# Splitting the weight conversion into parts that are queued behind subtractions and masks, deferring the split of group 2's x, and sharing the decays of k between two engines

## The chip, the core and the metric

The kernel runs on one core of one Trainium2 chip. The metric is the device time of one execution in microseconds. TensorE (PE) multiplies matrices, VectorE (DVE) and ScalarE (ACT) do elementwise work, GpSimd (POOL) does little here, and nearly all transfers are issued from SyncE's queue (SP). Each engine takes its instructions in order.

## The reference

Two stages follow each other. The first is a retention layer: per batch and head a 64 x 64 state decays by gamma in every step, takes in an outer product of k and v, and is read by q. The second is a feed-forward block with Silu on the 3072 tokens that come out.

```python
batch, n_heads, seq, head_dim = (4, 8, 768, 64)
gamma = 1.0 - 2.0 ** (-5.0 - np.arange(H))
for t in range(S):
    state = gamma * state + einsum('bhd,bhde', k[:, :, t], v[:, :, t])
    y[:, :, t] = scale * einsum('bhd,bhde->bhe', q[:, :, t], state)
h = x @ w_in                 # 3072 x 512 by 512 x 2048
out = (h * sigmoid(h)) @ w_out
```

The listing is shortened; q, k and v are float32 and the two weights are float64.

## The kernel before

**Units and visits.** The sequence is cut into 6 chunks of 128 tokens. A unit n is a pair of chunk c and batch b, n = 4c + b, and there are 24. `visit(m)` does three steps of a pipeline: it transposes k and q of unit m (`stage_t`, with copies out of PSUM on ScalarE at L338), computes scores and state products of unit m-1 (`stage_s`, `stage_a`, `finish_a`, `scale_q`), and the output y of unit m-2 (`stage_y`, `finish_y`). In `finish_a` VectorE multiplies the scores by a mask of decays (am, L370), and forms mid and the new state (L378, L382). `scale_q` multiplies the transposed q by its decays gq (L327). When a chunk begins, `next_chunk` multiplies gq by a step on GpSimd (L276). `scale_k` multiplies k by its decays: for units below 12 as eight pieces of 64 columns on ScalarE (L316), from 12 on as one instruction on VectorE (L320).

**Splits.** A float32 operand is multiplied as three parts (high, scaled low, and a mixed one), so each product of x and w is three matmuls per 128 rows. The four units of a chunk make one group c of x, 512 tokens. `finish_y` copies y out of PSUM (ys, L429, on ScalarE, for groups 0 to 2), and `split_x` makes the three parts: one on ScalarE (L440), two on VectorE (L443, L444). Group 2's ys are also written to memory (yd, L431), because its x is built a second time later.

**Weights.** w_in comes in 16 slices w_0 to w_15 (128 columns each), w_out in 16 more. A slice is loaded as 64-bit words (`load_w`, two slices ahead, in two buffers), and `convert_w` turns it into float32: ScalarE takes an absolute value (ca, L192), VectorE does six steps (L194, L196, L199, L201, L203, L206; here cs, ca, cs, cp, cp and the last add). `split_w` then makes three parts: wi on ScalarE (L116), wil on VectorE (L118), wi on ScalarE (L120), wi on VectorE (L121). `take_w` runs both for the next slice.

**Products.** `product_in(c, f)` multiplies group c with slice f: eight matmuls into bank ha and four into hb. ScalarE copies ha (L512), VectorE subtracts hb (L513), ScalarE applies Silu (L517), and `put_g` writes g to memory one product later. The g tiles and the ys tiles share three buffers (tag hs). The PSUM banks for ha, hb and for the transposed k come from a ring of three (`turn`), so a new transpose of k waits until the L513 that read the bank three turns earlier is done.

**Order.** Visits 0 to 9 come first, with slice 0 taken after visit 3 and slice 1 after visit 7. Then come the products (0,f) and (1,f) for f = 0 to 3; slice f+2 is taken at each (0,f), and visit 10+f follows (1,f). This makes four "periods" of two products and one visit. After them come (0,f), (1,f), (2,f-4) in turn, then the rest. TensorE's order is written out by hand as in the program; on the other engines a recording layer orders what is recorded, and `tc.issue_after` keeps instructions behind a named one. `held`, `evac`, `copied` and `taken_out` hold the last x rounding, transposed copy, ha copy and subtraction, to be named there.

**Output stage.** From about 375 us on, g is read back, split, and multiplied with w_out: for each of the six groups, 16 slices f by four batches b, three matmuls each, gm to ob, gh and glo to oa. A group ends with L648 (ScalarE copies ob) and L653 (VectorE scales oa and subtracts the copy), and a store. All eight banks are used by one group, so the next group's first matmuls wait for these.

Of the kernel before, what the change touches and what calls it, by code (L numbers as in the profile page):

```python
# [12 lines left out]
FP32 = mybir.dt.float32  # L13
# [18 lines left out]
def kernel(  # L32
# [77 lines left out]

    def split_w(f, w32, name, factor):

        w = w_slot(f, name)
        lo = conv.tile([128, 512], FP32, tag="wl", name=f"{name}l_{f}")
        with tc.issue_after(held[0] if f >= NF - 4 else evac[0]):
            nc.scalar.activation(out=w[:, 0, :], in_=w32, func=AF.Copy, scale=HALF * factor)  # L116
        high = w[:, 0, :].bitcast(FP32)
        nc.vector.scalar_tensor_tensor(out=lo, in0=w32, scalar=factor, in1=high,  # L118
                                       op0=ALU.mult, op1=ALU.subtract)
        nc.scalar.activation(out=w[:, 1, :], in_=lo, func=AF.Copy, scale=1.0 / EPS)  # L120
        nc.vector.scalar_tensor_tensor(out=w[:, 2, :], in0=high, scalar=EPS, in1=lo,  # L121
                                       op0=ALU.mult, op1=ALU.subtract)
        return w

# [46 lines left out]
    def convert_w(i):  # L171
# [12 lines left out]
        if not wide:  # L184
            return t
        words = t.rearrange("p (c w) -> p c w", w=2)
# [4 lines left out]
        with tc.issue_after(evac[0]) if evac else ExitStack():  # L191
# [12 lines left out]
                                       in1=p.bitcast(FP32), op0=ALU.mult, op1=ALU.mult)  # L204
        w = s.bitcast(FP32) if i < NF else conv.tile([128, DM], FP32, tag="wl", name=f"cw_{i}")
        nc.vector.tensor_tensor(out=w, in0=s.bitcast(FP32), in1=p.bitcast(FP32), op=ALU.add)  # L206
        return w

    evac, held, w_sb = [], [], {}
    taken = [0]  # L210

    def take_w(after=None):
        i = taken[0]
        taken[0] += 1
        if i >= 2 * NF:
            return
        with tc.issue_after(after) if after else ExitStack():
            w32 = convert_w(i)
        if i < NF:
            w_sb[i] = split_w(i, w32, "wi", scale)  # L220
        else:
            nc.sync.dma_start(out=wo_dram[i - NF], in_=w32)

# [51 lines left out]
    def next_chunk():  # L275
        nc.gpsimd.tensor_tensor(out=gq, in0=gq,  # L276
                                in1=step[:, :HP].unsqueeze(2).to_broadcast([128, HP, C]),
                                op=ALU.mult)


    xt, kt, qt, am = {}, {}, {}, {}
    behind_next = []
    taken_out, copied = [], []
    state, steps_of = {}, {}
# [23 lines left out]
    def scale_k(n):  # L308
        if 0 <= n < len(units):
            t = kqv["k"][n]  # L310
            if units[n][0] == NC - 1:
                t = t[:D]
            if n < 3 * B:

                for h in range(H):
                    nc.scalar.activation(out=t[:, h, :], in_=t[:, h, :], func=AF.Copy,  # L316
                                         scale=gk[:, units[n][0], h : h + 1])
                return
            g = gk[: t.shape[0], units[n][0], :].unsqueeze(2).to_broadcast([t.shape[0], H, D])
            nc.vector.tensor_tensor(out=t, in0=t, in1=g, op=ALU.mult)  # L320

    def scale_q(n):
        c, b = units[n]
        if c > 0 and b == 0:
            next_chunk()
        t, g = (x if c > 0 else x[:, :, D:] for x in (qt[n], gq))
        nc.vector.tensor_tensor(out=t, in0=t, in1=g, op=ALU.mult)  # L327
# [38 lines left out]
    def finish_a(n, sc, sums):  # L366

        c, b = units[n]
        am[n] = one.tile([128, 2, HP, D], FP32, tag="am", name=f"am_{n}")
        mask = nc.vector.tensor_tensor(out=am[n], in0=sc, in1=decay, op=ALU.mult).ins  # L370
        mid = one.tile([128, HP, D], FP32, tag="mid", name=f"mid_{n}", bufs=2)
        steps_of[n] = state.get(b), mid

        with tc.issue_after(mask):
            if c == 0:
                nc.scalar.copy(out=mid, in_=sums[:, 0])
            else:
                nc.vector.tensor_tensor(out=mid, in0=state[b], in1=sums[:, 0], op=ALU.add)  # L378
            if c < NC - 1:
                state[b] = one.tile([128, HP, D], FP32, tag="state", name=f"state_{n}",  # L380
                                    bufs=B + 2)
                nc.vector.tensor_tensor(out=state[b], in0=mid, in1=sums[:, 1], op=ALU.add)  # L382
# [51 lines left out]
    def split_x(c, b, y, raw):  # L434
        x = [xt[c][:, i, :, ts(b, C)] for i in range(3)]
        if raw is None:
            xh, xl = (t.rearrange("p a (o t) -> p o a t", o=2) for t in x[:2])
        else:
            (xh, xl), y = x[:2], raw
        held[:] = [nc.scalar.activation(out=xh, in_=y, func=AF.Copy, scale=HALF).ins]  # L440

        def rest():
            nc.vector.tensor_tensor(out=xl, in0=y, in1=xh.bitcast(FP32), op=ALU.subtract)  # L443
            nc.vector.scalar_tensor_tensor(out=x[2], in0=x[1].bitcast(FP32),  # L444
# [3 lines left out]

        if c > LATE:
            behind_next.append(rest)  # L450
        else:
            rest()
# [18 lines left out]
    def visit(m):  # L471

        first, mid, last = (0 <= m - i < len(units) for i in range(3))
        if first:
            stage_t(m)
# [8 lines left out]
        if mid:  # L484
            stage_a(m - 1, sc)
            with tc.issue_after(taken_out[0]) if taken_out else ExitStack():
                finish_a(m - 1, sc, sums)
            scale_q(m - 1)
        if m == 0:
# [14 lines left out]
    def product_in(c, f):  # L504
# [9 lines left out]
        with tc.issue_after(taken_out[0]):  # L514
            while behind_next:
                behind_next.pop()()
        nc.scalar.activation(out=hs, in_=hs, func=AF.Silu)  # L517
# [27 lines left out]
    def w_out(f):  # L545
        wo[f] = split_w(f, w_got.pop(f), "wo", 1.0)
        get_w(f + 2)
# [25 lines left out]
    for m in range(EARLY + 2):  # L573
        visit(m)
        if m in (3, 7):
            take_w()

# [24 lines left out]
    for n, (c, f) in enumerate(steps):  # L602
        product_in(c, f)
        if (c, f) in takes:
            take_w(taken_out[0] if n >= len(pairs + three) else None)
        put_g(1)
# [15 lines left out]
    for c in range(NC):  # L622
# [8 lines left out]
        for f in range(NF):  # L631
# [6 lines left out]
            for b in range(B):  # L638
                gh, glo, gm = (t[:, i, ts(b, C)] for i in range(3))
                oa, ob = acc[b]  # L640
                nc.tensor.matmul(ob, lhsT=gm, rhs=wo[f][:, 2, :], start=first_, stop=last)  # L641
                nc.tensor.matmul(oa, lhsT=gh, rhs=wo[f][:, 0, :], start=first_, stop=False)  # L642
                nc.tensor.matmul(oa, lhsT=glo, rhs=wo[f][:, 1, :], start=False, stop=last)  # L643
        for b in range(B):
            oa, ob = acc[b]
            o = one.tile([128, DM], FP32, tag=("kt", "qt")[b % 2], name=f"o_{c}_{b}",
                         bufs=(2, 3)[b % 2])
            nc.scalar.copy(out=o, in_=ob)  # L648

            n = 2 if (c, b) == (NC - 1, B - 1) else 1  # L650
            for i in range(n):
# [3 lines left out]
                                               op1=ALU.subtract)  # L655
                queue = nc.sync if c == NC - 1 else nc.scalar
                queue.dma_start(out=out[ds(b * S + c * C, C), cols], in_=o[:, cols])

# [29 lines left out]
```

## Time and profile before

The kernel took 645.5 us (median of 8 runs, 644.44 to 648.83). The profiled execution took 645.66 us; its span, first to last instruction, is 642.9 us, and the mean granted TensorE clock 0.991.

| | busy us | share of the span |
|---|---|---|
| PE | 614.1 | 96% |
| weight loads (PEld) | 507.6 | 79% |
| DVE | 420.2 | 65% |
| ACT | 308.9 | 48% |
| POOL | 11.8 | 2% |

The page's second part cuts the span into 40 slices of 16.1 us, where a digit is a share in tenths. A window view gives, for a stretch of time, each engine's busy time and the granted clock (1.00 is full speed). A timeline row reads: start, length, engine, line, operation, output <- input, and in brackets how long the engine sat idle before it and what released it. A row's length includes the time until its result is written, so two rows in succession overlap a little; what an engine can do per microsecond is read from the distance between starts. Idle time of an engine that does not set the end costs nothing.

| where | us |
|---|---|
| TensorE waits for the q of unit 8 until | 43.24 |
| product (0,0) starts | 54.91 |
| product (0,1) | 64.63 |
| product (0,2) | 73.25 |
| product (0,3) | 83.76 |
| product (0,4) | 97.53 |
| last matmul of the program starts | 637.97 |

### The profile page before, as it was taken

The numbers are of one execution on the slowest core, as the hardware profiler recorded it, in microseconds if no ns is written. First come the engines' busy times: TensorE is split into PE (matmuls) and PEld (weight loads), VectorE is DVE, ScalarE is ACT, GpSimd is POOL, SyncE is SP. The second block draws the span as 40 slices with busy tenths as digits, with TensorE's granted clock in tenths as the row PEclk, the third lists the DMA queues.
The fourth block names the chain that finished last, engine by engine and source line by source line (L and its number), as shares of the span: only waits on it lengthen the run. The fifth ranks groups of instructions, "written<-read, shape, count | busy, mean of one in ns | idle before, by whom it ended". The sixth has DMA issues, their size and how long they took to land.

```text
span 642.9 us, 13556 instructions
## 1 busy us (share of the span) xinstructions
PE 614.1 (96%) x5440; PEld 507.6 (79%) x5440; DVE 420.2 (65%) x725; ACT 308.9 (48%) x618; POOL 11.8 (2%) x70
## 2 busy tenths in 40 slices
PE   5787979999999999999999999999999999999997
PEld 3676767888888888888877888888788888888885
DVE  1788799769987766666789787364554635464631
ACT  7987766656755455444465884231312221322311
POOL 2100000000000000000000000000000000000000
PEclk9998989999999999999999999999999999999999
DMA  9986878536586756665468674243342524332301
GB/s 200 195 184 163 233 185 239 164 125 192 169 257 163 217 161 199 187 196 180 164 227 269 209 229 133 97 157 105 120 142 66 186 77 132 131 117 81 131 0 66
DMA packets 123215, 103.65 MB, mean 161 GB/s; under 512 B 80016, under 2 KB 88464, under 8 KB 123152
## 3 DMA queue, kind: packets, MB, share of 16 engines
q1 hardware_dynamic: 120272, 97.54, 52.2%
q10 hardware_dynamic: 2880, 5.24, 2.2%
q8 instruction: 42, 0.69, 0.5%
q14 instruction: 21, 0.17, 0.1%
HBM read 66.06 MB, written 36.70 MB: 160 GB/s over the span
## 4 chain that ended last, share of the span: by engine, by line
PE 80%; DVE 6%; ACT 5%; SPq 4%; DMA 2%; issue 2%; ACTq 0%; DVEq 0%; POOLq 0%
PE ha L508 25%; PE hb L508 12%; PE oa L642 6%; PE o L642 6%; PE o L643 6%; PE o L641 6%; PE oa L643 6%; PE ob L641 6%; SPq L144 3%; PE y L394 2%; DVE o L653 2%; PE sc L362 1%; ACT o L648 1%; PE sc L352 1%; ACT kf L316 1%
## 5 line engine op out<-in xcount | busy, mean ns | idle before, releaser
L508 PE MATMUL ha<-xt,wi 128*128 128x512 f32 x768 | 192.3, 392 | 0.7 <-DVE g L513 0.7
L508 PEld LDWEIGHTS ha<-xt,wi 128*128 128x128 f32 x768 | 142.6, 188 | 31.8 <-DVE g L513 1.5
L562 DVE TENSOR_TENSOR gs<-gr,gs 128x512 fp32r<-128x512 f32 x96 | 62.2, 685 | 87.4 <-ACT gs L560 87.4
L560 ACT ACTIVATE gs<-gr 128x512 fp32r<-128x512 f32 x96 | 53.6, 621 | 130.7 <-issue 130.0
L508 PE MATMUL hb<-xt,wi 128*128 128x512 f32 x384 | 103.1, 390 | 0.8 <-ACT g L512 0.8
L513 DVE TENSOR_TENSOR g<-g,hb 128x512 f32<-128x512 f32 x96 | 65.6, 684 | 43.4 <-ACT g L512 31.5
L517 ACT ACTIVATE g<-g 128x512 f32<-128x512 f32 x96 | 60.7, 633 | 64.9 <-DVE g L513 64.8
L508 PEld LDWEIGHTS hb<-xt,wi 128*128 128x128 f32 x384 | 71.6, 188 | 16.9 <-ACT g L512 1.8
L642 PE MATMUL oa<-wo,gs 128*128 128x512 f32 x192 | 75.4, 393 | 0.6 <-DVE o L653 0.2
L642 PE MATMUL o<-wo,gs 128*128 128x512 f32 x192 | 74.8, 389 | 0.0
L643 PE MATMUL oa<-wo,gs 128*128 128x512 f32 x192 | 74.7, 389 | 0.0
L641 PE MATMUL o<-wo,gs 128*128 128x512 f32 x192 | 74.7, 389 | 0.0
L643 PE MATMUL o<-wo,gs 128*128 128x512 f32 x192 | 74.7, 389 | 0.0
L641 PE MATMUL ob<-wo,gs 128*128 128x512 f32 x192 | 74.7, 389 | 0.0
L512 ACT ACTIVATE g<-ha 128x512 f32<-128x512 f32 x96 | 56.8, 592 | 31.3 <-PE ha L508 25.2
L563 DVE SCALAR_TENSOR_TENSOR gs<-gs 128x512 fp32r<-128x512 f32 x96 | 62.1, 683 | 0.0
L642 PEld LDWEIGHTS oa<-wo,gs 128*128 128x128 f32 x192 | 36.0, 188 | 10.1 <-DVE o L653 2.6
L641 PEld LDWEIGHTS ob<-wo,gs 128*128 128x128 f32 x192 | 36.0, 188 | 7.7
L641 PEld LDWEIGHTS o<-wo,gs 128*128 128x128 f32 x192 | 36.0, 188 | 7.6
L643 PEld LDWEIGHTS o<-wo,gs 128*128 128x128 f32 x192 | 36.0, 188 | 7.6
L642 PEld LDWEIGHTS o<-wo,gs 128*128 128x128 f32 x192 | 36.0, 188 | 7.5
L643 PEld LDWEIGHTS oa<-wo,gs 128*128 128x128 f32 x192 | 36.0, 188 | 7.3
(81 smaller groups left out, 665.8 us busy)
## 6 DMA issues: line engine op xcount, KB each, us to landing
gd<-g SPq DMA_DIRECT2D x96, 256.0 KB, 2.9
gr<-gd SPq DMA_DIRECT2D x96, 256.0 KB, 2.7
wf<-in_moe_w_out_dram SPq DMA_DIRECT2D x16, 512.0 KB, 3.9
out_dram<-o ACTq DMA_DIRECT2D x20, 256.0 KB, 2.1
wf<-in_moe_w_in_dram SPq DMA_DIRECT2D x16, 256.0 KB, 3.6
wf<-in_moe_w_in_dram SPq DMA_DIRECT2D x32, 128.0 KB, 3.9
kf<-in_k_dram SPq DMA_DIRECT2D x16, 256.0 KB, 5.4
qf<-in_q_dram SPq DMA_DIRECT2D x16, 256.0 KB, 4.6
```

The lines of the kernel that those rows point to most:

```text
L144: nc.sync.dma_start(out=t, in_=src[b, :, ds(c * C, C)].rearrange("h t d -> t h d"))
L394: i = nc.tensor.matmul(yp[ts(e, D), o, a, :], lhsT=lhsT, rhs=rhs, start=(e, o) not in started, stop=True, skip_group_check=True).ins
L508: nc.tensor.matmul(hb if i == 2 else ha, lhsT=w_sb[f][:, i, ts(kk, 128)], rhs=xt[c][:, i, kk, :], start=kk == 0 and i != 1, stop=kk == KIN ...
L512: copied[:] = [nc.scalar.activation(out=hs, in_=ha, func=AF.Copy, scale=ONE_E).ins]
L513: taken_out[:] = [nc.vector.tensor_tensor(out=hs, in0=hs, in1=hb, op=ALU.subtract).ins]
L517: nc.scalar.activation(out=hs, in_=hs, func=AF.Silu)
L560: nc.scalar.activation(out=t[:, 0, :], in_=g, func=AF.Copy, scale=HALF)
L562: nc.vector.tensor_tensor(out=t[:, 1, :], in0=g, in1=high, op=ALU.subtract)
L563: nc.vector.scalar_tensor_tensor(out=t[:, 2, :], in0=t[:, 1, :].bitcast(FP32), scalar=-1.0 / EPS, in1=high, op0=ALU.mult, op1=ALU.add)
L641: nc.tensor.matmul(ob, lhsT=gm, rhs=wo[f][:, 2, :], start=first_, stop=last)
L642: nc.tensor.matmul(oa, lhsT=gh, rhs=wo[f][:, 0, :], start=first_, stop=False)
L643: nc.tensor.matmul(oa, lhsT=glo, rhs=wo[f][:, 1, :], start=False, stop=last)
```

## The change

It has six parts.

1. `split_w` becomes a generator that pauses before its first VectorE step, and the last add of `convert_w` becomes a function of its own. `take_w` has a new argument: with parts = 2 (the periods) the last add and the first rounding are put in a list that runs behind the next subtraction, and the rest behind the next mask; with parts = 1 (the following products up to (2,3)) add and split run behind the next subtraction; with 0 all runs at once as before.
2. Slice 1 is taken after visit 8 instead of 7, behind the mask of that visit.
3. The two VectorE parts of group 2's x are also put behind the next subtraction.
4. The k of units 0, 2, 4 and 6 is scaled on VectorE, that of 12 and 13 on ScalarE; n = 1, 3, 5, 7 and 8 to 11 stay on ScalarE.
5. `next_chunk` runs on ScalarE, in four pieces of 128 columns, at the start of the visit.
6. In the output stage, for all groups but the last, the three matmuls come in the order oa, oa, ob; ScalarE copies and scales oa, and VectorE subtracts ob.

```diff
-    def split_w(f, w32, name, factor):
+    def split_w(f, w32, name, factor, to):
-        w = w_slot(f, name)
+        to[f] = w = w_slot(f, name)
...
         high = w[:, 0, :].bitcast(FP32)
+        yield
         nc.vector.scalar_tensor_tensor(out=lo, in0=w32, scalar=factor, in1=high,
...
-        return w
...
+        def rounded():
+            w = (s.bitcast(FP32) if i < NF else
+                 conv.tile([128, DM], FP32, tag="wl", name=f"cw_{i}"))
+            nc.vector.tensor_tensor(out=w, in0=s.bitcast(FP32), in1=p.bitcast(FP32), op=ALU.add)
+            return w
+
+        return rounded
...
-    def take_w(after=None):
+    def take_w(after=None, parts=0):
...
         with tc.issue_after(after) if after else ExitStack():
-            w32 = convert_w(i)
-        if i < NF:
-            w_sb[i] = split_w(i, w32, "wi", scale)
+            rounded = convert_w(i)
+
+        def finish():
+            w32 = rounded()
+            if i < NF:
+                split = split_w(i, w32, "wi", scale, w_sb)
+                if parts == 2:
+                    next(split)
+                    behind_mask.append(split)
+                else:
+                    list(split)
+            else:
+                nc.sync.dma_start(out=wo_dram[i - NF], in_=w32)
+
+        if parts:
+            behind_next.append(finish)
         else:
-            nc.sync.dma_start(out=wo_dram[i - NF], in_=w32)
+            with tc.issue_after(after) if after else ExitStack():
+                finish()
...
     def next_chunk():
-        nc.gpsimd.tensor_tensor(out=gq, in0=gq,
-                                in1=step[:, :HP].unsqueeze(2).to_broadcast([128, HP, C]),
-                                op=ALU.mult)
+        for a in range(HP):
+            nc.scalar.activation(out=gq[:, a, :], in_=gq[:, a, :], func=AF.Copy,
+                                 scale=step[:, a : a + 1])
...
-            if n < 3 * B:
+            if n in (1, 3, 5, 7) or 2 * B <= n < 3 * B + 2:
...
         mask = nc.vector.tensor_tensor(out=am[n], in0=sc, in1=decay, op=ALU.mult).ins
+        masked[:] = [mask]
...
-        if c > LATE:
+        if c > LATE or c == LATE and y is not None:
             behind_next.append(rest)
...
+        if mid and m > 1 and units[m - 1][1] == 0:
+            next_chunk()
...
+            with tc.issue_after(masked[0]):
+                while behind_mask:
+                    list(behind_mask.pop(0))
             scale_q(m - 1)
...
-                behind_next.pop()()
+                behind_next.pop(0)()
...
-        if m in (3, 7):
-            take_w()
+        if m in (3, EARLY):
+            take_w(masked[0] if m == EARLY else None)
...
-            take_w(taken_out[0] if n >= len(pairs + three) else None)
+            take_w(taken_out[0], 2 if n < len(pairs) else int(n < len(pairs + three)))
...
+                todo = [(oa, gh, 0), (oa, glo, 1), (ob, gm, 2)]
+                for o, g, i in todo if c < NC - 1 else todo[2:] + todo[:2]:
+                    nc.tensor.matmul(o, lhsT=g, rhs=wo[f][:, i, :], start=first_ and i != 1,
+                                     stop=last and i != 0)
...
+            if c < NC - 1:
+                nc.scalar.activation(out=o, in_=oa, func=AF.Copy, scale=ONE_E)
+                nc.vector.tensor_tensor(out=o, in0=o, in1=ob, op=ALU.subtract)
+                nc.scalar.dma_start(out=out[rows, :], in_=o)
+                continue
```

## The prediction

> **What bounds it now.** First the 40 slices of 16.1 us on the page:
>
> ```profile
> PE   5787979999999999999999999999999999999997
> DVE  1788799769987766666789787364554635464631
> PEclk9998989999999999999999999999999999999999
> ```
>
> TensorE is at nine tenths or more from slice 7 on, so time can be won almost only before about 108 us. Next, who TensorE waits for before 130 us:
>
> ```profile
> PE kp L336 <- DMA kqv<-in_k_dram: 5.1, 3, 2.2
> ...
> PE kp L336 <- DVE g L513: 3.7, 2, 3.1
> PE y L394 <- ACT ys L429: 3.3, 2, 2.5
> ...
> PE hb L508 <- ACT g L512: 0.8, 1, 0.8
> ```
>
> (us in all, times, longest.) DMA waits belong to the opening, where loads arrive one after another; the others are queueing in VectorE and ScalarE. Third, the stretches between the first and the fifth product of group 0 (start:end, length, then busy us of PE, PEld, DVE, ACT, POOL; granted clock, DMA share, GB/s):
>
> ```profile
> 48.00:54.90 6.90, 3.93 (x132) 3.45 (x130) 5.81 (x11) 5.69 (x15) 1.13 (x2) 0.75 0.86 195
> 54.90:64.60 9.70, 8.83 (x168) 7.35 (x160) 8.66 (x17) 6.99 (x12) 0.09 (x1) 1.00 0.56 142
> 64.60:73.25 8.65, 8.65 (x167) 7.38 (x160) 6.82 (x13) 6.09 (x18) 0.09 (x1) 1.00 0.78 219
> 73.25:83.76 10.51, 9.14 (x167) 7.23 (x161) 9.19 (x18) 7.87 (x19) 0.09 (x1) 1.00 0.72 198
> 83.76:97.53 13.77, 10.55 (x166) 8.69 (x160) 12.67 (x23) 7.88 (x15) 1.13 (x2) 0.88 0.82 209
> ```
>
> A period is two products (4 x 1.36 us each, that is 5.44) and a visit (3.05 from the undisturbed one, 70.20 to 73.25): 8.5 us. The second period achieves that, the fourth takes 13.8, because VectorE is late there. Fourth, the timelines of VectorE and of TensorE at that stall (start, length, then the wait in brackets):
>
> ```profile
> 89.34 1.42 DVE L443 TENSOR_TENSOR xt<-ys,xt 128x512 fp32r<-128x512 f32 x1
> 90.68 0.68 DVE L203 SCALAR_TENSOR_TENSOR cp<-wf,cp 128x512 f32<-128x512 uint32 x1
> 91.28 0.68 DVE L444 SCALAR_TENSOR_TENSOR xt<-xt 128x512 fp32r<-128x512 f32 x1
> 91.89 0.67 DVE L513 TENSOR_TENSOR g<-g,hb 128x512 f32<-128x512 f32 x1
> ```
> ```profile
> 92.61 1.12 PE L336 MATMUL kp<-ident,kf 128*128 128x128 f32 x4 [3.11 <-DVE g L513]
> ```
>
> The L513 subtraction of (0,3) had its matmuls by 86.8 but stood behind mask, state, decays, a split and a conversion step. It frees the PSUM bank of the next transposes, so TensorE sat 3.11 us. A shorter such case: at 50.90 the y products waited 2.49 us for an L429 copy queued on ScalarE behind w_1's two roundings (L116, L120), which waited for VectorE.
>
> **What is there to win.** The five waits after 47 us are 2.49, 0.48 (L352 for L382), 0.79, 0.58 and 3.11: 7.45 us. Then the clock. The Trainium skill (TensorE: Matmul & The Clock Gate, What's actually happening) ties the half clock to about 3.4 us of idleness; by that alone these gaps cost nothing more. The trace differs: after the 2.49 and 3.11 us gaps the granted clock was 0.57 in 50.90 to 54.91 and 0.55 in 92.61 to 96.00. The visit at 92.61 took 4.92 instead of 3.05 us (1.87 lost), the one at 50.90 took 4.01 from its y products on where 71.17 to 73.25 took 2.08 (1.93, of it 0.48 counted). So 3.3 more by the row, 10.8 together; I take the row.
>
> **Part by part.**
> *Anchor.* The first 35 issues on the SP queue keep their order. At 43.24 TensorE waits for the q of unit 8 by DMA (0.60), so nothing before 43.24 can come earlier; I keep the visit there, with its 1.14 us of issue, to 47.31. Four k scalings moved to VectorE here (n = 0, 2, 4, 6) save ScalarE 8 steps, 1.9 us, and cost VectorE 0.60 each: both before the anchor or beside loads, worth 0; without that cover at most 0.60 each.
>
> *w_1 taken one visit later, behind the mask.* Its conversion leaves the visits of 42 to 50 us: the ys copy then follows the y products at once and the mask of unit 7 comes at 47.1 instead of 49.62. Gone: 2.49 and most of 0.48 and of 1.93. The visit takes 3.05 and some slack: (0,0) starts at 51.3 instead of 54.91, 3.6 won. Given back: between the state of unit 7 (ends near 49.0) and the last split of unit 7's x, VectorE now has 16 instructions. By the distance of their starts in its timeline (91.28 to 91.89 for one) they are eleven of 0.60, two of 0.33, cs 0.34, ca 0.42 and cp 0.43: 8.45, and 8.7 with some 0.1 between dependent neighbours (80.51 to 81.23). They end at 57.7; product (1,0) wants that third part at 51.3 + 2.72 + 1.81 = 55.8. So TensorE ends (1,0) at 57.7 + 0.91 = 58.6 instead of 60.54: 1.9 left. The w_3 load on SP also no longer stands 4.9 us (for L203 at 47.66) ahead of k, q of unit 10 and v of 9; these come 6 us earlier, which is slack.
>
> *Slices in parts, halves of group 2's x.* No operation and no semaphore is added, only order: what waits behind the mask is wil, and behind the next subtraction the splits of x, needed a period or more later ((2,0) is the first reader of x of group 2). The ys tile is held some 3 us longer, and is wanted again only by the next visit's ys. In the built order VectorE goes mask, mid, wil, state, wi, q decay, subtraction (0,f), split, cs, split, ca, cs, subtraction (1,f), cp, cp, last add. Ahead of the L513 of (0,f) stand now 0.60 + 0.33 + 0.69 + 0.33 + 0.60 + 0.60 = 3.2 us after the mask may start, which is about the length of the end of the visit and one product: no stall of 3.11. The period's list is again those lengths, two subtractions in place of two of the splits: 8.7 us, against TensorE's 8.5: **VectorE becomes the pace**, with TensorE just behind it. What it waits for: the ha copy on ScalarE. ScalarE has in a period copies 3 x 0.47, rounding and Silu 5 x 0.53, ca 0.56, k 1.92, ha 2 x 0.47: some 7.5 us, 8.9 with the gq of one.
>
> *gq on ScalarE.* POOL's L276 took 1.04 at 51.92 and 89.17; L443 beside it took 1.42, against 0.68 elsewhere: 0.74 each, 1.5 of VectorE saved after the anchor. On ScalarE: 4 pieces of 128x128, by the L273 row 1.26 us in all (the decays of the first chunk). It queues ahead of the qt copy and the Silu, none of which ends a TensorE wait within 1.3 us; if it did, 1.3 per chunk, five times, of which three lie in the TensorE-bound part with ScalarE half idle (50.30 of 100 us busy from 200 to 300).
>
> *k of units 12 and 13 to ScalarE.* The skill (ScalarE: Activation LUTs, Rules for kernel authors) says to use VectorE for a multiply, which speaks against this: 1.92 us for 0.60. By the rule the sum loses 2 x 1.3 us. By the rows VectorE was busy 12.67 of 13.77 us in the fourth period and ScalarE 7.88; so I count 1.2 us off VectorE, and nothing for ScalarE, whose k must only be ready a visit later.
>
> *Output stage.* At each of the five changes of group an oa of the fourth batch waits for its L653. Near 420 us that row runs from 420.23 to 420.92, because ScalarE's copy for that batch (419.61) stands behind three stores; the matmul starts 0.49 after the one before it, the next 0.34, where 0.23 is usual: 0.37 lost. In the new order both oa want ScalarE's copy, over at 420.10, and only the third matmul wants VectorE, at 420.49 + 0.46 = 420.95, when it is just done: 0.35 won at four changes. The last group keeps ob first, so there VectorE's end delays the first of the three: 0.2 more lost. That is 1.2 won; bounds -0.5 (VectorE late by another split) and 1.4. The tail is unchanged.
>
> **Sum.** Starts of (0,f): (0,1) at 58.6 + 3.05 + 0.3 = 62.0. Then three periods: at least 8.7 by VectorE; at most like the old mean, (97.53 - 64.63)/3 = 11.0, if ordering does nothing. I take 9.4, nearer the lower end because the old second period did 8.6 with the same engines, with 0.7 left for a late ha copy or a DMA landing. (0,4) starts at 62.0 + 28.2 = 90.2 instead of 97.53: 7.3. From there TensorE is the bound and everything moves with it; (2,0) needs the last split of unit 11 at once, for which 0.5 us is taken off. 7.3 - 0.5 + 1.2 = 8.0 us. The profiled execution ran 645.66 (642.9 span and 2.8 around it), 0.16 over the median, so 637.7 for it, and 637.5 for the median.
>
> **Rivals.**
> 1. *The other engines do not follow*: periods of 10 to 11 us. For it: ScalarE's order has the ys copy behind the k pieces and a rounding, and Silu's table load of 1.28 stands there. Against: it idled 5.15 us in the old fourth period. (0,4) at 62.0 + 31.5 = 93.5, 4.0 - 0.5 + 1.2 = 4.7 won: 640.8.
> 2. *All of it at the TensorE pace*: (1,0) in time and 8.5 a period gives (0,4) at 51.3 + 34.0 = 85.3, 12.2 won and 1.2 in the output stage: 632.1. Against: VectorE's 8.7 with no idle, where it idled some 5 us in the old 50.
> 3. *It does not do what it says*: the stalls move from the subtraction to the xl of unit 7, w_1 and the last add, as long as before, and the output stage wins what it wins: 644.3 to 645.5, say 645. Against: what stood ahead of L513 really is shorter.
> 4. *Slower*: the g and ys buffers. The three hs tiles turn once a period; the copy of ha(1,f+1) needs the put of g(1,f), which the SP queue issues behind yd and a v load. In the old second period that copy waited 1.16 us (ACT g L512 for the yd landing, 71.62). With shorter periods the put, at visit end + 1.7 to 3, lands 2.9 to 4.6 later, against 4.5 us available. ScalarE then blocks, VectorE's next subtraction and mask too. Decisive when each landing is 4 us late: a 3.1 us stall and 1.5 of slow clock each time, 4.6 x 3 on 8.7-us periods gives (0,4) at 102, 4.4 later, 1.2 back: 648.7. Against: only 1.16 occurred at 0.78 DMA share.
>
> **Chances and range.** Forecast (6 to 11 won, 634.5 to 639.5) 0.60; rival 1 (2 to 6 won) 0.17; rival 2 0.09; rival 3 0.07; rival 4 0.07. This kernel's runs spread from 644.44 to 648.83; about 0.3% (1.9 us) is what can be told from no change. So faster 0.86, same 0.07, slower 0.07. The range runs from 633.5, into rival 2 by some of its chance, to 642.5, which takes in most of rival 1.
>
> **What would show it.** Right: no TensorE wait on L429 near 48; (0,0) near 51.3; a wait of (1,0) for the last split near 55.8; no kp wait over 1 us; VectorE above nine tenths from 50 to 88; L465 near 0.68 with POOL free of L276; (0,4) near 90; clock 1.00 in all periods; no matmul 0.49 after another near the changes of group but one. Wrong: a q8 landing much later than 43.2, ScalarE waiting for a DMA ahead of the ha copy, or a period above 10.5 us.

## The result, and the profile after

In alternating runs the changed kernel took 640.63 us (median of 12, 638.24 to 644.71), the kernel before 646.26 us (33 runs). The ratio is 0.9916 (95% interval 0.9898 to 0.9934): 0.84% faster, 5.6 us. 637.5 was forecast from a median of 645.5, that is 8.0 won. Of the 3.1 us between forecast and result, 0.8 is that the kernel before itself ran at 646.26 in these runs; 2.4 is gain that did not come. The profiled execution has a span of 637.3 us, against 642.9.

Line numbers have shifted. The products are now L535, the ha copy L539 (was L512), the subtraction of hb L540 (L513), ys L450 (L429), the splits of x L465 and L466 (L443, L444), the mask L390 (L370), y L415 (L394), the two roundings of a slice L117 and L122.

The 40 slices of the page of the changed kernel:

```profile
PE   5778999999999999999999999999999999999997
DVE  1769898889978666666788797463644544554631
PEclk9999999999999999999999999999999999999999
```

TensorE is at nine tenths or more from slice 5 on (64 us), where it was slice 7 (96 us), and the granted clock is at nine tenths or more in every slice. Who TensorE waits for before 130 us (total, times, longest):

```profile
PE kp L356 <- DMA kqv<-in_k_dram: 8.4, 4, 4.3
PE y L415 <- issue: 5.3, 6, 1.8
PE y L415 <- ACT ys L450: 2.0, 2, 1.2
PE ha L535 <- issue: 1.3, 1, 1.3
...
PE sc L382 <- issue: 0.9, 1, 0.9
PE hb L535 <- ACT g L539: 0.7, 1, 0.7
```

Both long waits on queues are gone: 2.49 us on the ys copy, and 3.11 on the subtraction; the two waits on ys that are left lie before 36 us. What has appeared is the word "issue": time in which the profile shows nothing that TensorE waited for. It comes to 8.4 us before 130 us, against 3.0 in the kernel before. The stretches from product (0,0) to (0,4) show the periods (start:end, length, then PE, PEld, DVE, ACT, POOL busy; clock, DMA share, GB/s):

```profile
52.55:63.73 11.18, 9.03 (x165) 7.36 (x160) 10.39 (x20) 9.22 (x19) 0.09 (x1) 1.00 0.54 141
63.73:72.61 8.88, 8.80 (x167) 7.41 (x161) 7.69 (x15) 7.59 (x21) 0.34 (x1) 1.00 0.86 237
72.61:81.59 8.98, 8.95 (x167) 7.30 (x161) 8.10 (x16) 6.95 (x18) 0.09 (x1) 1.00 0.80 223
81.59:92.19 10.60, 9.23 (x167) 7.49 (x161) 9.52 (x19) 10.34 (x28) 0.09 (x1) 1.00 0.80 216
```

The second and third periods run at TensorE's pace (8.80 of 8.88 and 8.95 of 8.98 us busy). The fourth, 13.77 us before, takes 10.60, and its fullest helper is no longer VectorE but ScalarE (10.34 us). VectorE's timeline in the fourth period, from the mask to the subtraction that caused the 3.11 us stall:

```profile
83.06 0.68 DVE L390 TENSOR_TENSOR am<-sc,decay 128x512 f32<-128x512 f32 x1
83.66 0.41 DVE L399 TENSOR_TENSOR mid<-state,sc 128x256 f32<-128x256 f32 x1
83.99 0.68 DVE L120 SCALAR_TENSOR_TENSOR wil<-cs,wi 128x512 f32<-128x512 f32 x1
84.59 0.41 DVE L403 TENSOR_TENSOR state<-mid,sc 128x256 f32<-128x256 f32 x1
84.92 0.69 DVE L123 SCALAR_TENSOR_TENSOR wi<-wi,wil 128x512 fp32r<-128x512 f32 x1
85.52 0.68 DVE L347 TENSOR_TENSOR qt<-qt,gq 128x512 f32<-128x512 f32 x1
87.11 0.69 DVE L540 TENSOR_TENSOR g<-g,hb 128x512 f32<-128x512 f32 x1 [0.91 <-ACT g L539]
```

From mask to the end of the q decay it is 3.14 us (3.2 was forecast; before, 4.41 from mask to subtraction), and then VectorE **idles 0.91 us for ScalarE's copy of ha**.

Where the gain stands along the way, by the starts in TensorE's timelines of the two profiled executions:

| at | before | after | gain |
|---|---|---|---|
| (0,0) | 54.91 | 52.55 | 2.4 |
| (0,1) | 64.63 | 63.73 | 0.9 |
| (0,4) | 97.53 | 92.19 | 5.3 |
| (2,0) | 103.51 | 97.76 | 5.8 |
| first output matmul | 374.72 | 369.70 | 5.0 |
| last matmul | 637.97 | 632.35 | 5.6 |

### The profile page after: what moved, and what is told of

It is laid out like the page before. It is cut to its first block, busy times and chain, and to the rows that moved or that the text cites. A ratio compares the mean times of both kernels' runs of the same rounds, so it can differ in the third digit from the quotient of the medians.

```text
span 637.3 us, 13569 instructions
## 1 busy us (share of the span) xinstructions
PE 610.8 (96%) x5440; PEld 504.5 (79%) x5440; DVE 419.4 (66%) x727; ACT 312.4 (49%) x622; POOL 7.0 (1%) x65
## 5 line engine op out<-in xcount | busy, mean ns | idle before, releaser
L535 PE MATMUL ha<-xt,wi 128*128 128x512 f32 x768 | 192.5, 392 | 1.8 <-issue 1.3
L535 PEld LDWEIGHTS ha<-xt,wi 128*128 128x128 f32 x768 | 142.6, 188 | 33.1 <-DVE g L540 1.5
L671 PE MATMUL o<-wo,gs 128*128 128x512 f32 x576 | 146.3, 389 | 0.0
L671 PE MATMUL oa<-wo,gs 128*128 128x512 f32 x384 | 118.3, 389 | 0.1
L535 PE MATMUL hb<-xt,wi 128*128 128x512 f32 x384 | 103.4, 391 | 0.9 <-ACT g L539 0.9
L540 DVE TENSOR_TENSOR g<-g,hb 128x512 f32<-128x512 f32 x96 | 65.6, 684 | 41.1 <-ACT g L539 33.5
L535 PEld LDWEIGHTS hb<-xt,wi 128*128 128x128 f32 x384 | 71.6, 188 | 17.6 <-ACT g L539 2.5
L539 ACT ACTIVATE g<-ha 128x512 f32<-128x512 f32 x96 | 56.8, 591 | 30.0 <-PE ha L535 24.4
L390 DVE TENSOR_TENSOR am<-sc,decay 128x512 f32<-128x512 f32 x24 | 16.5, 688 | 17.1 <-PE sc L382 17.1
L193 ACT ACTIVATE ca<-wf 128x512 f32<-128x512 f32 x32 | 21.5, 673 | 10.8 <-DMA wf<-in_moe_w_out_dram 4.8
L200 DVE SCALAR_TENSOR_TENSOR cs<-ca,cs 128x512 uint32<-128x512 uint32 x32 | 22.1, 690 | 0.8
L204 DVE SCALAR_TENSOR_TENSOR cp<-wf,cp 128x512 f32<-128x512 uint32 x32 | 22.1, 690 | 0.8
L679 ACT ACTIVATE o<-o 128x512 f32<-128x512 f32 x10 | 6.0, 600 | 33.1 <-PE o L671 32.7
L415 PE MATMUL y<-qt,mid 64*64 64x64 f32 x384 | 21.1, 225 | 0.0
```

What stands on the lines that cost most here:

```text
L193: nc.scalar.activation(out=a.bitcast(FP32), in_=hi.bitcast(FP32), func=AF.Abs, scale=65536.0)
L200: nc.vector.scalar_tensor_tensor(out=s, in0=a, scalar=3, in1=s, op0=ALU.logical_shift_left, op1=ALU.bitwise_or)
L204: nc.vector.scalar_tensor_tensor(out=p.bitcast(FP32), in0=lo, scalar=2.0 ** -52, in1=p.bitcast(FP32), op0=ALU.mult, op1=ALU.mult)
L415: i = nc.tensor.matmul(yp[ts(e, D), o, a, :], lhsT=lhsT, rhs=rhs, start=(e, o) not in started, stop=True, skip_group_check=True).ins
L535: nc.tensor.matmul(hb if i == 2 else ha, lhsT=w_sb[f][:, i, ts(kk, 128)], rhs=xt[c][:, i, kk, :], start=kk == 0 and i != 1, stop=kk == KIN ...
L539: copied[:] = [nc.scalar.activation(out=hs, in_=ha, func=AF.Copy, scale=ONE_E).ins]
```

## The experiments

Eight kernels ran. My first theory was the one on record: slices in parts and the deferral of x together remove the 3.11 us stall. Rivals: that another part of the change does it, and that the missing gain is lost to transfers. All the ratios are to the kernel before, run in alternation; its median was 646.26 us beside the change, 645.93 beside the next four kernels and 647.33 beside the last four, so ratios are compared and not times. "Three periods" is the time from (0,1) to (0,4), which leaves the opening out; the three starts are from TensorE's timeline of one profiled execution of each kernel.

| kernel | ratio (95%) | (0,0) | (0,1) | (0,4) | three periods |
|---|---|---|---|---|---|
| before | 1 | 54.91 | 64.63 | 97.53 | 32.9 |
| the change | 0.9916 (0.9898 to 0.9934) | 52.55 | 63.73 | 92.19 | 28.5 |
| u_parts | 0.9925 (0.9904 to 0.9946) | 51.75 | 62.67 | 92.01 | 29.3 |
| u_w1 | 0.9929 (0.9907 to 0.9951) | 55.66 | 64.96 | 93.49 | 28.5 |
| u_gq | 0.9941 (0.9920 to 0.9961) | 53.39 | 65.11 | 93.55 | 28.4 |
| u_k1213 | 0.9920 (0.9899 to 0.9942) | 52.13 | 63.05 | 92.32 | 29.3 |
| u_out | 0.9907 (0.9873 to 0.9941) | 50.62 | 61.82 | 90.97 | 29.2 |
| rows2k_before | 1.0031 (1.0001 to 1.0060) | 55.20 | 67.92 | 102.66 | 34.7 |
| rows2k_after | 1.0049 (1.0019 to 1.0078) | 51.97 | 63.99 | 97.48 | 33.5 |
| late_wi_last | 0.9874 (0.9841 to 0.9907) | 52.53 | 62.90 | 91.29 | 28.4 |

u_out gives the measure of what one profile can tell: it is the changed kernel up to the output stage, and yet its (0,0) and (0,1) start 1.9 us earlier than in the other profile, and its three periods take 0.7 longer. Smaller differences of these starts between two profiles say nothing, and none of the ratios of single undone parts stands clear of the change's own interval. Part 3 of the change (the deferral of group 2's x) and the first half of part 4 (k of units 0, 2, 4 and 6) were not undone in any run.

### Slices whole again

```diff
-            take_w(taken_out[0], 2 if n < len(pairs) else int(n < len(pairs + three)))
+            take_w(taken_out[0] if n >= len(pairs + three) else None)
```

> The changed kernel with the slices from w_2 on converted whole again, as before; all else changed. My theory: the order in parts is what brought the subtraction L513 forward in the third and fourth periods, where the start of (0,4) won 4.4 of its 5.3 us ((0,2) had won 0.6 to 0.9). Then about 4 us are lost again, 0.998 of the kernel before, and a wait of the transposes for the subtraction returns. Rival: freeing VectorE (gq off GpSimd, k of 12 and 13 on ScalarE) did it; then at most 1 us is lost, 0.993.

Measured 641.04 us, 0.9925: nothing that can be told from the change. **My first theory fell here**: I had expected most of the fourth period's gain to go. VectorE's timeline of this kernel around the same subtraction:

```profile
82.73 0.69 DVE L390 TENSOR_TENSOR am<-sc,decay 128x512 f32<-128x512 f32 x1
...
85.12 0.69 DVE L200 SCALAR_TENSOR_TENSOR cs<-ca,cs 128x512 uint32<-128x512 uint32 x1
85.85 0.43 DVE L202 TENSOR_SCALAR cp<-cs 128x512 uint32<-128x512 uint32 x1
87.15 0.69 DVE L540 TENSOR_TENSOR g<-g,hb 128x512 f32<-128x512 f32 x1 [0.88 <-ACT g L539]
87.76 0.69 DVE L465 TENSOR_TENSOR xt<-ys,xt 128x512 fp32r<-128x512 f32 x1
88.36 0.69 DVE L204 SCALAR_TENSOR_TENSOR cp<-wf,cp 128x512 f32<-128x512 uint32 x1
88.96 0.69 DVE L466 SCALAR_TENSOR_TENSOR xt<-xt 128x512 fp32r<-128x512 f32 x1
```

With the slice whole, VectorE has other conversion steps ahead of L540, but it is again through 0.9 us before ScalarE's copy is there. What is not ahead of it is the pair L465, L466 and the cp between them. In the kernel before, these three stood at 89.34, 90.68 and 91.28, just ahead of the subtraction at 91.89: 2.55 us, of which 0.74 is the collision of the first with GpSimd. The mask of that period also comes earlier: 1.6 us after the start of (0,3) here, 3.7 us in the kernel before,

```profile
87.48 0.68 DVE L370 TENSOR_TENSOR am<-sc,decay 128x512 f32<-128x512 f32 x1
```

so 2.1 us were backlog from the third period, in which a scaling of k (L320, at 83.51) is among the steps. With the slices whole (here), gq on GpSimd, or k of 12 and 13 on VectorE, each undone alone, the three periods take 28.4 to 29.3 us instead of 32.9, so none of these parts is needed for the gain while the others stand. This leaves the deferral of group 2's x as the likeliest cause. A kernel with the deferral alone undone, and one with it alone done, did not run: that it is the cause, and that no two of the other parts together would do, is argued from the traces and not shown.

### Slice 1 after visit 7 again

```diff
-        if m in (3, EARLY):
-            take_w(masked[0] if m == EARLY else None)
+        if m in (3, 7):
+            take_w()
```

> The changed kernel with slice 1 taken after visit 7 again. Prediction: the wait of 2.49 us on the ys copy returns, minus the 1.7 given back: 1.9 us lost, 0.9945 of the kernel before. Rival: with w_1 late, the SP queue no longer stops for the w_3 load, so the loads of units 10 and 11 run at 43 to 50 us and slow TensorE's fetch of instructions (its idle time put down to issue: 1.33, 0.99 and 1.28 us); with w_1 early these waits shrink, 0.9 us or less is lost, 0.9925 or so.

Measured 641.65 us, 0.9929. The wait returns: TensorE's waits between 36 and 64 us hold

```profile
PE y L415 <- issue: 2.5, 2, 1.8
PE y L415 <- ACT ys L450: 2.4, 1, 2.4
PE sc L372 <- DVE state L403: 0.6, 1, 0.6
```

and the windows around it show the clock fall after it:

```profile
52.00:53.00 1.00, 0.59 (x32) 0.45 (x32) 1.00 (x3) 1.00 (x3) 0.00 (x0) 1.00 0.94 207
53.00:54.00 1.00, 0.78 (x40) 0.78 (x44) 0.97 (x3) 1.00 (x4) 0.00 (x0) 0.83 1.38 266
54.00:55.00 1.00, 1.00 (x51) 1.00 (x47) 0.50 (x1) 1.00 (x5) 0.09 (x1) 0.50 1.21 208
```

(0,0) starts at 55.66, 3.1 us later than in the change's profile (3.6 was forecast). So the placing of slice 1 removes the wait on ys, as the prediction says. How much of that is given back before (0,1) the profiles don't settle: there u_w1 is 1.2 us behind the change's profile and 3.1 behind u_out's. At the end it is 1.0 us (641.65 less 640.63), within the intervals. The rival's forecast, shorter issue waits, is half there: the waits of 0.99 and 1.28 us of the change are absent, those before them are 1.77 and 0.78.

### gq on GpSimd again, and k of units 12 and 13 on VectorE again

```diff
     def next_chunk():
-        for a in range(HP):
-            nc.scalar.activation(out=gq[:, a, :], in_=gq[:, a, :], func=AF.Copy,
-                                 scale=step[:, a : a + 1])
+        nc.gpsimd.tensor_tensor(out=gq, in0=gq,
+                                in1=step[:, :HP].unsqueeze(2).to_broadcast([128, HP, C]),
+                                op=ALU.mult)
```

> The changed kernel with the decays gq on GpSimd again, at the new place. Prediction: L465 or another VectorE row beside it grows by 0.5 to 0.8 each, 0.8 to 1.5 us lost in the two chunks after 43 us: 0.9935. Rival: ScalarE, not VectorE, ends the waits of the periods (the subtraction waited 0.8 to 1.1 for the ha copy in each), and without 1.27 us of gq it is earlier in the fourth period: 0 to 0.7 us won, 0.991.

Measured 642.79 us, 0.9941, the largest loss of a single part, though its interval still overlaps the change's. In the timeline of VectorE the contention is back at one of two places only: beside the GpSimd instruction of 49.95 to 50.99

```profile
50.11 1.16 DVE L195 TENSOR_SCALAR cs<-wf 128x512 uint32<-128x512 uint32 x1
51.19 0.68 DVE L465 TENSOR_TENSOR xt<-ys,xt 128x512 fp32r<-128x512 f32 x1
```

where L195 takes 0.42 elsewhere: 0.74 more, the same 0.74 as in the kernel before (1.42 for 0.68). It is followed by a wait of 1.06 us of (1,0) for the split at 58.18, in TensorE's timeline:

```profile
58.92 1.21 PE L535 MATMUL ha<-xt,wi 128*128 128x512 f32 x4 [1.06 <-DVE xt L465]
```

Of the delay of that split 0.74 us is the collision; another 0.6 is a step of the slice (L123) that stands ahead of it in this kernel and behind it in the change. The second GpSimd instruction (87.08 to 88.12) meets VectorE waiting for ScalarE's copy and then in its subtraction at 87.93, which takes the usual 0.69 us: it costs nothing. The three periods are as short as in the change (28.4), so gq's engine is not what shortened them.

```diff
-            if n in (1, 3, 5, 7) or 2 * B <= n < 3 * B + 2:
+            if n in (1, 3, 5, 7) or 2 * B <= n < 3 * B:
```

> The changed kernel with the k of units 12 and 13 on VectorE again. Prediction: VectorE is the pace, 1.2 us more of it: up to 1.2 us lost, 0.9935. Rival: ScalarE is the pace (it waits for nothing between 74 and 77 us and so copies ha 1.7 us after it is ready); without two times 1.92 us it is earlier, and 0.5 to 1 us is won, 0.990.

Measured 640.69 us, 0.9920: the change's time. VectorE has room for the two decays: it idles 1.58 and 0.81 us for ScalarE's copy in the second and third period, and in the fourth its subtraction follows at 86.38 without a wait.

### The output stage as before

The edit puts back the order ob, oa, oa and the copy of ob on ScalarE for all groups, and the store that goes with them.

```diff
-                for o, g, i in todo if c < NC - 1 else todo[2:] + todo[:2]:
+                for o, g, i in todo[2:] + todo[:2]:
...
-            if c < NC - 1:
-                nc.scalar.activation(out=o, in_=oa, func=AF.Copy, scale=ONE_E)
-                nc.vector.tensor_tensor(out=o, in0=o, in1=ob, op=ALU.subtract)
-                nc.scalar.dma_start(out=out[rows, :], in_=o)
-                continue
```

> The changed kernel with the output stage of before. Prediction: 1.2 us lost, 0.9935 of the kernel before. By the two traces only 0.6 was won between the first output matmul (5.02 us ahead) and the last (5.62 ahead): then 0.9925, and at each of five changes of group a matmul 0.49 and one 0.34 after the one before.

Measured 639.98 us, 0.9907: no loss that the times can show. Inside the traces the stage from its first matmul to its last takes 263.1 us here (369.47 to 632.58) and 262.65 in the change: the new order is worth 0.46 us where 1.2 was forecast. TensorE's timeline at a change of group shows why, first with the old order, then with the new one:

```profile
415.13 0.39 PE L671 MATMUL ob<-wo,gs 128*128 128x512 f32 x1
415.62 0.72 PE L671 MATMUL oa<-wo,gs 128*128 128x512 f32 x2
416.18 1.55 PE L671 MATMUL o<-wo,gs 128*128 128x512 f32 x6
```
```profile
415.62 0.62 PE L671 MATMUL oa<-wo,gs 128*128 128x512 f32 x2
416.13 0.50 PE L671 MATMUL ob<-wo,gs 128*128 128x512 f32 x1
416.46 1.54 PE L671 MATMUL o<-wo,gs 128*128 128x512 f32 x6
```

Starts are 0.23 us apart when nothing delays them. Old: 0.49 for one and 0.56 for two, 0.36 lost. New: 0.51 for two and 0.33 for one, 0.15 lost. So 0.2 instead of 0.35 is won at a change of group; with four of these it is 0.8, of which the last change gives back a part, as in the changed kernel an ob waits 0.35 us there for VectorE's L680 (at 590.96).

### Larger rows for q, k and v

Transfers were suspected of two things: of the issue waits, and of late landings (rival 4 of the prediction). To change the transfers alone, q, k and v of units 8 to 23 were loaded in rows of 2 KB in place of 256 bytes, in both kernels; these units then see the tokens in another order.

```diff
-        nc.sync.dma_start(out=t, in_=src[b, :, ds(c * C, C)].rearrange("h t d -> t h d"))
+        if n < EARLY:
+            nc.sync.dma_start(out=t, in_=src[b, :, ds(c * C, C)].rearrange("h t d -> t h d"))
+        else:
+            nc.sync.dma_start(out=t.rearrange("p h d -> p (h d)"), in_=src[b, :, ds(c * C, C)].rearrange("h (p r) d -> h p (r d)", r=H))
```

> The kernel before with q, k and v of units 8 to 23 loaded in rows of 2 KB instead of 256 bytes: as many bytes in an eighth of the pieces; tokens and columns come out in another order, so this computes something else with the same instructions on all engines. It tells how much the load of the DMA engines costs. If the loads pace only the visits up to 8 (prediction): q of unit 8 comes earlier by 1 us or more, but the waits on queues remain, so 0 to 1 us is won. If instruction fetch behind the loads costs time: TensorE's issue waits at 40, 45 and 64 us (0.95, 1.14, 0.87) get shorter too, 1 to 3 us won.

> The same loads in the changed kernel. If the changed kernel lost part of its gain to instruction fetch behind the earlier loads (my theory for the 1.7 us missing at (0,1)): the issue waits of 1.33, 0.99 and 1.28 us between 46 and 55 us vanish or halve, and it wins 2 to 3.5 us, more than the kernel before does with the same loads. Rival, that these waits have another cause (the place in the instruction buffer alone): they stay, and at most 1 us is won.

Measured 649.52 us (1.0031) on the kernel before and 649.85 us (1.0049) on the changed one: both slower, and by the medians the change is worth nothing there. In the two profiles the changed kernel is 5.2 us ahead at (0,4) and 1.6 at the last matmul. Of its three issue waits, those of 1.33 and 0.99 us vanish and the one of 1.28 becomes 1.01, as my theory asked, but no time is won, so this run can't confirm the theory. ScalarE's waits from 50 to 100 us in rows2k_after:

```profile
ACT g L542 <- DMA gd<-g: 4.6, 2, 3.0
ACT g L542 <- DMA yd<-ys: 4.1, 1, 4.1
```

L542 is this kernel's copy of ha. It needs a buffer that a put of g or ys still reads. TensorE then waits for the copy:

```profile
74.20 2.11 PE L538 MATMUL ha<-xt,wi 128*128 128x512 f32 x8 [1.51 <-ACT g L542]
80.81 1.20 PE L538 MATMUL hb<-xt,wi 128*128 128x512 f32 x4 [1.78 <-ACT g L542]
85.77 2.11 PE L538 MATMUL ha<-xt,wi 128*128 128x512 f32 x8 [0.81 <-ACT g L542]
92.38 1.20 PE L538 MATMUL hb<-xt,wi 128*128 128x512 f32 x4 [1.77 <-ACT g L542]
```

The first and third of these are on copies that a put held up (at 73.55 and 85.12). The other two are on the next copies (at 80.18 and 91.75), which waited for no transfer themselves but stand behind 6.6 us of ScalarE's work that began late; the change has such a wait too, of 0.71 us, without a late put in that period. So rival 4's mechanism is real: late puts cost 2.3 us directly and up to 5.9 with what follows, and the three periods take 33.5 instead of 28.5. In the change itself it stayed at one wait of 1.04 us (for yd, at 79.86), which reached nothing on TensorE.

### The second rounding of a slice behind the ha copy

The change's own profile shows ScalarE as the last to arrive. This version moves L122 behind the next copy of ha, and gives the last output group the order oa, oa, ob for all slices but the last.

```diff
+        low = lambda: nc.scalar.activation(out=w[:, 1, :], in_=lo, func=AF.Copy, scale=1.0 / EPS)
+        if later is None:
+            low()
...
+        if later is not None:
+            later.append(low)
...
+        with tc.issue_after(copied[0]):
+            while behind_copy:
+                behind_copy.pop(0)()
...
-                for o, g, i in todo if c < NC - 1 else todo[2:] + todo[:2]:
+                for o, g, i in todo if (c, f) != (NC - 1, NF - 1) else todo[2:] + todo[:2]:
```

> The changed kernel with two further edits: the last ScalarE rounding of a slice (L122) is queued behind the next ha copy, and the last group takes the order oa, oa, ob but for its last slice. If ScalarE's late ha copy is what ends the waits of the periods: the subtraction (0,f) comes 0.5 earlier in each, the wait of 0.71 for hb in the fourth period goes, 0.5 to 1.2 us won, and 0.4 more at the last change of group (0.51 and 0.33 after the one before): 0.990. If VectorE is the pace: only the 0.4, 0.991.

Measured 638.82 us (636.88 to 640.96), 0.9874 (0.9841 to 0.9907): the fastest of all, though its interval still overlaps the change's at the edge. ScalarE's timeline in the fourth period has the two in the new order, the copy (now L543) first:

```profile
85.06 0.58 ACT L543 ACTIVATE g<-ha 128x512 f32<-128x512 f32 x1
85.54 0.62 ACT L122 ACTIVATE wi<-wil 128x512 fp32r<-128x512 f32 x1
```

and TensorE's wait for it falls from 0.71 to 0.16 us. But an issue wait in the same period rises from 0.65 to 1.18 in this profile, so the three periods stay at 28.4, and the forecast gain there did not come. The span is 2.2 us shorter than the change's: 0.8 at (0,1), another 0.9 between (0,4) and the first output matmul (at 367.93 instead of 369.70), and 0.4 in the output stage (262.3 us instead of 262.65). The first two are within what two profiles of one program differ by: u_out and the change are 1.0 us apart in the stretch from (0,4) to the output stage. What of the gain is the edit's own is thus not shown.

## Why the prediction was right, and where its sum was off

**The direction and the place were right.** The time was won before 100 us, where the two queueing stalls stood, and it was carried to the end. That the first stall went by moving slice 1 is shown by u_w1. Which part removed the second is not shown: the prediction credited the parts and the deferral together, and u_parts leaves the deferral.

**Anchor.** Forecast: TensorE waits for the transfer of unit 8's q until 43.24, so nothing before that can come earlier. Measured: TensorE took it up at 43.88 in the change and at 42.47 in u_out, in neither after a wait for that transfer. In the change the issue wait ahead of it had grown to 1.77 us (at 41.37) from 0.95. So the transfer did not fix this point; the issue waits moved it.

**Slice 1 later.** (0,0) at 51.3 forecast, 52.55 measured (50.62 in u_out). The wait on ys is gone. Two issue waits stand in its place, which the kernel before and u_w1 don't have:

```profile
50.47 0.63 PE L415 MATMUL y<-am,kqv 64*64 64x64 f32 x27 [0.99 <-issue]
54.57 1.52 PE L535 MATMUL ha<-xt,wi 128*128 128x512 f32 x6 [1.28 <-issue]
```

They cost nothing at (0,1), because VectorE came last, as forecast: it was busy 8.47 of the 8.54 us from the end of unit 7's state (49.96) to the end of the last split of its x (58.50), and hb of (1,0), which needs that split, came right behind:

```profile
57.82 0.68 DVE L466 SCALAR_TENSOR_TENSOR xt<-xt 128x512 fp32r<-128x512 f32 x1
58.65 1.16 PE L535 MATMUL hb<-xt,wi 128*128 128x512 f32 x4
```

(0,1) came at 63.73 instead of 62.0, and **this is where the sum was mis-sized**, by two terms. VectorE's list took 8.5 us, 8.7 forecast, but began at 49.96 instead of 49.0, as the opening's issue waits came to 1.77 and 1.33 us instead of 0.95 and 1.14: the split was 0.8 late. And the visit behind (1,0) was put at 3.05 us and 0.3 of slack, the length of an undisturbed one, although the kernel before shows an issue wait of 0.87 in it (at 64.00): it stood there again, 0.88 at 63.11, and the way from hb to (0,1) took 5.1 us instead of 4.3. In u_out, whose opening ran earlier, (0,1) came at 61.82.

**The three periods.** Forecast 28.2 us, measured 28.46: right in size, by a reason that was half wrong, so in part by luck. "VectorE becomes the pace" did not happen: it was busy 87 to 90% of them and idled 0.8 to 1.1 us in each of the three for ScalarE's copy of ha. Two periods ran at TensorE's own pace, and the fourth lost 1.37 us to ScalarE (0.71) and issue (0.65). Two signs that the prediction had named for being wrong appeared, both small: the fourth period took 10.60 us (its limit was 10.5), and ScalarE waited 1.04 us for a transfer ahead of a copy of ha.

**gq and k.** L465 is at 0.68 throughout, as forecast. The loss from contention is confirmed as 0.74 per event, but it only costs where VectorE is the late one, once in u_gq. The two decays moved to ScalarE were counted as 1.2 us off VectorE; u_k1213 shows nothing that they are worth.

**(2,0).** 0.5 us was taken off for the last split of unit 11; instead 0.4 was won (the way from (0,4) to (2,0) is 5.57 us, before 5.98). From there to the output stage the lead shrinks from 5.75 to 5.02 us, which no step foresaw: 0.4 of it goes in one product near 340 us, in which TensorE waits 0.16 us for ScalarE's copy of ha. At the product behind, both kernels wait for the subtraction, 0.54 us at 347.56 and 0.42 before (at 352.76).

**Output stage.** 1.2 forecast; 0.6 between the two profiles, 0.46 between the change and u_out. The prediction had VectorE just done when the third matmul comes; 0.15 us is still lost at a change of group.

**The clock.** The prediction took the row over the rule of the Trainium skill (TensorE: Matmul & The Clock Gate, What's actually happening), which ties the half clock to about 3.4 us of idleness. The runs agree with the row: in u_w1 the clock was 0.50 from 54 to 55, after a gap of 2.36 us that ended at 51.90, and in the change, with no wait above 1.4 us after 42, it is 1.00 in every period. By the rule alone the stalls would have been worth 3.3 us less. When the clock falls the runs don't settle (see the last section).

**The sum.** Forecast: 2.6 at (0,1), 4.7 in the periods, -0.5, 1.2. Measured: 0.9, 4.4, then -0.3 between (0,4) and the output stage, 0.6. The 1.7 at (0,1) and the 0.6 in the output stage account for 2.3 of the 2.4 us. That the parts add up so well to the difference of the medians is partly luck: they are read from one profiled execution of each kernel, and those two differ by 5.6 us in span but by 6.6 in device time (645.66 and 639.03), while the runs of the change spread over 6.5.

**The rivals.** The result lands near rival 1's 640.8, but not by its mechanism: its periods were to be 10 to 11 us, and they are 9.5 on average. Against rival 2 the prediction held that VectorE idled some 5 us in the old 50; by its own five rows it is 6.4. Rival 4 did not occur in this kernel; rows2k_after shows what it costs when it does.

## What to carry to other kernels

When several parts of a change each take work from in front of the same late instruction, undoing one shows little, because the rest still suffice; read in the trace which instructions stood directly ahead of the late one, and test each alone as well as undone. When a stall is removed, the engines behind it are late by their own amounts, and waits that lay inside the stall come out: forecast which of them ends last, not the full length of the old one. A wait that the trace of the old kernel shows in a stretch belongs into the forecast of that stretch. Keep the instruction that frees TensorE's bank first in its engine's queue, and check which transfer must land before it.

## What the runs showed of the hardware that was not expected

- **The issue waits stand at fixed places, each behind a transfer of instructions.** In the change the matmuls behind such a wait start at 41.37, 46.21, 50.47, 54.57 and 63.11, and from one to the next lie 126 to 128 matmuls and 126 to 129 weight loads; the next wait, at 91.93, comes 510 matmuls later, four times 127. The other kernels with these waits have them at the same distances; in the kernel before 126 and 380 matmuls lie between the three at 40.14, 45.39 and 64.00. The page of the change has this row among the DMA queues (packets, MB, share):

```profile
q8 instruction: 43, 0.70, 0.5%
```

  That is 16 KB a packet, and one packet for 253 of the 10880 matmuls and weight loads. In the traces of before, the change, u_w1, u_gq, u_out and both kernels with larger rows, one of these packets moves 2.3 to 3.3 us before TensorE goes on, at every issue wait from 38 to 65 us. So TensorE most likely waits for its next block of instructions. In the kernel before and in u_w1 the packets moved at 47.05 and 47.65, and TensorE stood in its stall on ys until 50.90 and 51.90: no issue wait is left to see at that block. That the same program's (0,0) moved by 1.9 us from one profile to another (change and u_out) is largely the wait at 41.37, 1.77 and 0.67 us long.
- **What makes a block late stays open.** I suspected the loads of q, k and v, because the kernel before holds back its loads and has a DMA share of 0.10 from 46 to 49 us, where the change has 0.91. The runs don't settle it: with the larger rows the issue waits on y between 36 and 64 us fell to 0.2 us in the changed kernel, and rose to 3.1 in the kernel before.
- **The clock fell after two short waits as well.** In rows2k_after TensorE was busy 0.66 of the 2 us from 42 to 44 (waits of 0.57 and 0.79 us for loads), and from 46 to 48 us the clock was 0.50. But in u_w1 it was busy only 0.48 of the 2 us from 40 to 42 (a wait of 1.77 us), and the clock stayed at 1.00 until 53. So neither the length of one gap nor the busy share of 2 us tells these cases apart.
- **Larger rows did not help.** Rows eight times as long moved 8.70 MB from 50 to 100 us instead of 9.78 in the change, at a DMA share of 0.55 instead of 0.72, and ScalarE waited up to 4.1 us for a put. As the kernel with larger rows was also further back at 100 us, the smaller traffic is in part a consequence of the waits.
- **A GpSimd instruction of 1.04 us holds VectorE up for 0.74,** for an instruction with one input (1.16 for 0.42, in u_gq) as for one with two (1.42 for 0.68, in the kernel before). In both the VectorE instruction started 0.16 to 0.17 us after GpSimd's and ended its usual length after a point 0.13 to 0.14 us before GpSimd's end, as if it had stood still until then.
